# Score products on two 64-row halves of TensorE, with z turned by DMA transposes

## The chip, the cores and the metric

One core of one Trainium2 chip. The metric is the device time of one execution in microseconds (us). Executions of one kernel mostly agree within about 0.3%. Engines: PE is TensorE, DVE is VectorE, ACT is ScalarE, POOL is GpSimd, and SP issues the DMAs. PE writes its products to the memory PSUM; to empty PSUM means to read them from there with ACT or DVE, so that the buffer can be filled again.

## The reference

An attention unit with squared relu scores is followed by a mixer. The shapes are 8 batches, 3136 rows, width 256, and 64 columns of z.

```python
scores = (1 / S) * matmul(z, z.T)              # z: [8, 3136, 64]
x = u * matmul(maximum(scores, 0) ** 2, v)     # u, v: [8, 3136, 256]
h = x.T @ U @ V                                # rank 32
u2 = x + h.T
out = u2 + maximum(u2 @ w_ch1, 0) @ w_ch2      # 256 -> 1024 -> 256
```

## The kernel before

Rows are taken in 25 tiles of 128. For each batch, z is scaled to bf16 (z_bf, whose upper 64 columns are zero), turned on PE against an identity, and cast from PSUM to zzT by ACT. A score product contracts the 128 rows of zzT, of which 64 are zeros.

```python
z_bf = pb2.tile([P, NT, P], BF16, name="z_bf", bufs=1)
nc.gpsimd.memset(z_bf[:, :, dqk:], 0.0)
nc.scalar.mul(out=z_bf[:, :, :dqk], in_=z_raw, mul=zscale)
zzT = pb2.tile([P, S_pad], BF16, name="zzT")              # two buffers
for tg in range(0, NT, 4):
    ...                                                   # four products with ident, one ACT cast to zzT
```

Attention goes by groups of 512 rows (six, and one of 128). A pair of score tiles fills two PSUM banks and is emptied by a relu, one pair in four on DVE and the rest on ACT. DVE then squares it in SBUF. The products with v follow, 100 per group of 512.

```python
ps_s = ps2_pool.tile([P, 2, IGW], FP32, name="ps2")       # three buffers
for jj in range(npair):
    nc.tensor.matmul(out=ps_s[:, jj, :gw],
                     lhsT=zzT[:, (jp + jj) * P : (jp + jj + 1) * P],
                     rhs=zzT[:, g0 : g0 + gw], start=True, stop=True)
if (jp // 2) % 4 == 3:
    nc.vector.tensor_single_scalar(out=attn_sb[...], in_=ps_s[...], scalar=0.0, op=ALU.max)
else:
    nc.scalar.activation(out=attn_sb[...], in_=ps_s[...], func=AF.Relu)
nc.vector.tensor_tensor(out=attn_sb[...], in0=attn_sb[...], in1=attn_sb[...], op=ALU.mult)
```

The kernel is written batch by batch as attention(b), preparation of z and v for b+1, mixer(b). A scheduler sets the final order on each engine and moves work far ahead where buffers allow.

## Time and profile before

| | before |
|---|---|
| time | 1375.08 us |
| PE, DVE, ACT busy | 96%, 52%, 58% |
| attention of a batch (1 to 7), to the start of its last score product | 106.6 us |
| hand-over: from there to the first relu of the mixer (1 to 6) | 13.8 us |
| mixer, from there to its last product | 47.5 us |

The page of a profile gives shares over the whole span. A timeline line gives start, duration (of all merged instructions), engine, source line, operation, output and input, count, and in brackets the idle time before it with what ended it. The last three rows of the table are read from such starts. The lines themselves stand in the prediction.

### The profile page before, as it was taken

The page shows a single profiled execution, that of the slowest core. Times are in us where ns is not written, and L with a number is a line of the kernel's source. Part 1 is how long each engine was busy: PE and PEld are TensorE (multiplying, and loading weights), DVE is VectorE, ACT ScalarE, POOL GpSimd, SP SyncE. Part 2 cuts the span into 40 slices and gives each one's busy share as a digit, 9 for nine tenths or more (in the row PEclk, how much of TensorE's full clock was granted, in tenths as well). Part 3 has the DMA queues.
Part 4 walks back from the last instruction along what each step waited for, and adds up shares of the span by engine and source line. Part 5 has one row for each costly group of instructions (what it writes and reads, how often), then busy time and mean ns, then how long its engine had stood idle before and what let it go on. Part 6 is the DMA issues. An engine that isn't in the chain of part 4 may idle for free.

```text
span 1373.0 us, 22895 instructions
## 1 busy us (share of the span) xinstructions
PE 1317.1 (96%) x9865; PEld 913.3 (67%) x10008; DVE 707.9 (52%) x1104; ACT 792.9 (58%) x976; POOL 23.7 (2%) x41
## 2 busy tenths in 40 slices
PE   3999999999999999999999999999999999999998
PEld 1677666676666766667666676666766667666665
DVE  1776147751477414774157732677217772177721
ACT  6854855557555575556655565655655555455554
POOL 2000000000000000000000000000000000000000
PEclk9999999999999999999999999999999999999999
DMA  9611421124111241111411115111121111111101
GB/s 238 181 32 30 146 71 32 32 64 134 49 32 32 65 146 43 31 32 57 148 49 32 32 49 157 41 32 32 57 102 33 32 32 34 62 34 32 32 32 65
DMA packets 109542, 87.89 MB, mean 64 GB/s; under 512 B 32832, under 2 KB 109120, under 8 KB 109440
## 3 DMA queue, kind: packets, MB, share of 16 engines
q1 hardware_dynamic: 109440, 86.41, 20.7%
q8 instruction: 78, 1.28, 0.4%
q14 instruction: 24, 0.20, 0.0%
HBM read 60.70 MB, written 25.69 MB: 63 GB/s over the span
## 4 chain that ended last, share of the span: by engine, by line
PE 75%; ACT 21%; DMA 2%; issue 1%; DVE 1%; ACTq 0%; SPq 0%; POOL 0%
ACT relu_sb L277 12%; ACT attn_sb L184 4%; ACT u2T_bf L260 3%; ACT zzT L135 2%; DMA v_raw<-in_v_dram 1%; PE ps_6060 L202 0%; PE ps_4297 L202 0%; PE ps_11349 L202 0%; PE ps_7477 L202 0%; PE ps_2188 L202 0%; PE ps_12766 L202 0%; PE ps_11003 L202 0%; PE ps_9240 L202 0%; PE ps_5714 L202 0%; PE ps_2534 L202 0%
## 5 line engine op out<-in xcount | busy, mean ns | idle before, releaser
L202 PEld LDWEIGHTS <-attn_sb 128*128 128x128 bf16 x5000 | 466.9, 98 | 164.3 <-DVE attn_sb L189 61.9
L189 DVE TENSOR_TENSOR attn_sb<-attn_sb 128x1024 bf16<-128x1024 bf16 (+3 forms) x728 | 407.0, 608 | 73.7 <-ACT attn_sb L184 71.4
L169 PEld LDWEIGHTS <-zzT 128*128 128x128 bf16 x1400 | 133.3, 98 | 107.2 <-issue 29.3
L297 PEld LDWEIGHTS <-relu_sb 128*128 128x128 bf16 x1600 | 148.6, 98 | 50.5 <-ACT relu_sb L277 24.0
L270 PEld LDWEIGHTS <-w_bf 128*128 128x128 bf16 x896 | 83.2, 98 | 87.2 <-issue 7.8
L150 ACT CAST v_bf<-v_raw 128x1024 bf16<-128x1024 f32 (+1 forms) x56 | 52.0, 965 | 24.0 <-DMA v_raw<-in_v_dram 15.5
L246 PEld LDWEIGHTS <-x_bf 128*128 128x128 bf16 x400 | 30.3, 97 | 10.7 <-issue 4.5
L128 PEld LDWEIGHTS <-z_bf 128*128 128x128 bf16 x200 | 16.1, 102 | 26.3 <-issue 22.5
L289 PEld LDWEIGHTS <-V_bf 128*128 128x128 bf16 x200 | 19.3, 98 | 6.4
L223 PEld LDWEIGHTS <-U_bf 128*128 128x128 bf16 x200 | 19.6, 98 | 2.2
L212 POOL MEMSET u_sb<- 128x256 f32 x8 | 2.5, 311 | 1047.3 <-DVE x_bf L214 1047.3
L128 PE MATMUL ps_124<-ident,z_bf 128*128 128x128 bf16 x4 | 0.6, 299 | 19.7 <-ACT z_bf L121 19.7
L120 POOL MEMSET z_bf<- 128x1600 bf16 x8 | 11.4, 1431 | 80.8 <-PE ps_6732 L253 13.6
L121 ACT ACTIVATE z_bf<-z_raw 128x1600 bf16<-128x1600 f32 x8 | 12.4, 1550 | 0.0
L253 PEld LDWEIGHTS <-t_sb 128*128 128x128 bf16 x112 | 10.9, 97 | 1.4 <-issue 1.1
L305 DVE TENSOR_TENSOR out_sb<-ps_1522,x_bf 128x512 f32<-128x512 f32 x1 | 0.7, 692 | 16.8 <-PE ps_1522 L297 16.8
L305 DVE TENSOR_TENSOR out_sb<-ps_6811,x_bf 128x512 f32<-128x512 f32 x1 | 0.7, 692 | 16.7 <-PE ps_6811 L297 16.7
L305 DVE TENSOR_TENSOR out_sb<-ps_8574,x_bf 128x512 f32<-128x512 f32 x1 | 0.7, 692 | 16.7 <-PE ps_8574 L297 16.7
L305 DVE TENSOR_TENSOR out_sb<-ps_5048,x_bf 128x512 f32<-128x512 f32 x1 | 0.7, 690 | 16.7 <-PE ps_5048 L297 16.7
L305 DVE TENSOR_TENSOR out_sb<-ps_10337,x_bf 128x512 f32<-128x512 f32 x1 | 0.7, 692 | 16.7 <-PE ps_10337 L297 16.7
L305 DVE TENSOR_TENSOR out_sb<-ps_3285,x_bf 128x512 f32<-128x512 f32 x1 | 0.7, 690 | 16.7 <-PE ps_3285 L297 16.7
L305 DVE TENSOR_TENSOR out_sb<-ps_12100,x_bf 128x512 f32<-128x512 f32 x1 | 0.7, 690 | 16.7 <-PE ps_12100 L297 16.7
(2728 smaller groups left out, 2817.8 us busy)
## 6 DMA issues: line engine op xcount, KB each, us to landing
v_raw<-in_v_dram SPq DMA_DIRECT2D x48, 512.0 KB, 4.8
u_sb<-in_u_dram SPq DMA_DIRECT2D x96, 256.0 KB, 2.6
out_dram<-out_sb SPq DMA_DIRECT2D x96, 256.0 KB, 2.1
z_raw<-in_z_dram SPq DMA_DIRECT2D x8, 768.0 KB, 5.3
wtmp<-in_moe_w_ch_dram SPq DMA_DIRECT2D x4, 512.0 KB, 3.8
v_raw<-in_v_dram SPq DMA_DIRECT2D x8, 64.0 KB, 2.2
u_sb<-in_u_dram SPq DMA_DIRECT2D x8, 64.0 KB, 2.1
out_dram<-out_sb SPq DMA_DIRECT2D x8, 64.0 KB, 2.0
```

Source lines behind the costliest of these rows:

```text
L135: nc.scalar.copy(out=zzT[:, tg * P : (tg + n_in_g) * P], in_=pz[:, : n_in_g * P],)
L150: nc.scalar.copy(out=v_bf[:, c0 : c0 + cn, :], in_=v_raw[:, :cn, :])
L169: nc.tensor.matmul(out=ps_s[:, jj, :gw], lhsT=zzT[:, (jp + jj) * P : (jp + jj + 1) * P], rhs=zzT[:, g0 : g0 + gw], start=True, stop=True,)
L184: nc.scalar.activation(out=attn_sb[:, jp : jp + npair, :gw], in_=ps_s[:, :npair, :gw], func=AF.Relu,)
L189: nc.vector.tensor_tensor(out=attn_sb[:, jp : jp + npair, :gw], in0=attn_sb[:, jp : jp + npair, :gw], in1=attn_sb[:, jp : jp + npair, :gw] ...
L202: nc.tensor.matmul(out=ps_o[:, qq, :], lhsT=attn_sb[:, jt, q * P : (q + 1) * P], rhs=v_bf[:, jt, :], start=(jt == 0), stop=(jt == NT - 1),)
L223: nc.tensor.matmul(out=pt1[:, 0, :], lhsT=U_bf[:, it, :], rhs=x_bf[:, it, :], start=(it == 0), stop=(it == NT - 1),)
L246: nc.tensor.matmul(out=ps_u2[:, db, q * P : (q + 1) * P], lhsT=x_bf[:, it, db * P : (db + 1) * P], rhs=ident, start=(q == 0), stop=False,)
L260: nc.scalar.copy(out=u2T_bf[:, :, c0 : c0 + cw], in_=ps_u2[:, :, :cw])
L270: nc.tensor.matmul(out=ps_m1[:, hh, :cw], lhsT=w1_bf[:, db, ht * P : (ht + 1) * P], rhs=u2T_bf[:, db, c0 : c0 + cw], start=(db == 0), stop ...
L277: nc.scalar.activation(out=relu1_sb[:, hp : hp + 2, :cw], in_=ps_m1[:, :, :cw], func=AF.Relu,)
L297: nc.tensor.matmul(out=ps_f[:, qq, :], lhsT=relu1_sb[:, ht, q * P : (q + 1) * P], rhs=w2_bf[:, ht, :], start=False, stop=(ht == NH - 1),)
```

## The change

A score product needs only 64 rows of the array. The change puts z on both partition halves of zzT and computes the two tiles of a pair on the two halves of the array at the same time. The transposes leave PE and ACT for the DMA queue.

```diff
-        nc.gpsimd.memset(z_bf[:, :, dqk:], 0.0)
         nc.scalar.mul(out=z_bf[:, :, :dqk], in_=z_raw, mul=zscale)
-
+        nc.vector.tensor_copy(out=z_bf[:, :, dqk:], in_=z_bf[:, :, :dqk])
         zzT = pb2.tile([P, S_pad], BF16, name="zzT")
-        for tg in range(0, NT, 4):
-            (PE products with ident, ACT cast to zzT: 14 lines cut)
+        for h0 in range(0, NT, 13):
+            h1 = min(NT, h0 + 13)
+            nc.sync.dma_start_transpose(
+                out=zzT[:, h0 * P : h1 * P].rearrange("p (t r) -> p t r", r=P),
+                in_=z_bf[:, h0:h1, :].rearrange("p t c -> p (t c)"),
             )
...
-                        lhsT=zzT[:, (jp + jj) * P : (jp + jj + 1) * P],
-                        rhs=zzT[:, g0 : g0 + gw],
+                        lhsT=zzT[jj * 64 : jj * 64 + 64, (jp + jj) * P : (jp + jj + 1) * P],
+                        rhs=zzT[jj * 64 : jj * 64 + 64, g0 : g0 + gw],
```

More of the change, by code (lines that the diff above doesn't have):

```diff
@@ L119, in emit_prep @@
         z_bf = pb2.tile([P, NT, P], BF16, name="z_bf", bufs=1)
-        nc.gpsimd.memset(z_bf[:, :, dqk:], 0.0)
         nc.scalar.mul(out=z_bf[:, :, :dqk], in_=z_raw, mul=zscale)
+        nc.vector.tensor_copy(out=z_bf[:, :, dqk:], in_=z_bf[:, :, :dqk])
         zzT = pb2.tile([P, S_pad], BF16, name="zzT")
-        for tg in range(0, NT, 4):
-            n_in_g = min(4, NT - tg)
-            pz = ps1_pool.tile([P, 512], FP32, name="ps1")
-            for q in range(n_in_g):
-                nc.tensor.matmul(
-                    out=pz[:, q * P : (q + 1) * P],
-                    lhsT=z_bf[:, tg + q, :],
-                    rhs=ident,
-                    start=(q == 0),
-                    stop=(q == n_in_g - 1),
-                )
-            nc.scalar.copy(
-                out=zzT[:, tg * P : (tg + n_in_g) * P],
-                in_=pz[:, : n_in_g * P],
+        for h0 in range(0, NT, 13):
[3 more added lines that the diff above has]
+                in_=z_bf[:, h0:h1, :].rearrange("p t c -> p (t c)"),
             )
```

## The prediction

> **What bounds the kernel now.** I read the page first, for shares and for the chain that ended last, then the timeline of single engines over one stretch of attention, then the timeline of ACT where attention hands over to the mixer.
>
> ```profile
> PE 1317.1 (96%) x9865; PEld 913.3 (67%) x10008; DVE 707.9 (52%) x1104; ACT 792.9 (58%) x976; POOL 23.7 (2%) x41
> ...
> PE 75%; ACT 21%; DMA 2%; issue 1%; DVE 1%; ACTq 0%; SPq 0%; POOL 0%
> ACT relu_sb L277 12%; ACT attn_sb L184 4%; ACT u2T_bf L260 3%; ACT zzT L135 2%; DMA v_raw<-in_v_dram 1%; PE ps_6060 L202 0%; PE ps_4297 L202 0%; PE ps_11349 L202 0%; PE ps_7477 L202 0%; PE ps_2188 L202 0%; PE ps_12766 L202 0%; PE ps_11003 L
> ```
>
> This looks PE-bound: 96% busy and 75% of the chain. But the 96% is a count of overlapping, pipelined matmuls and hides a slack of some per cent, and 52% for DVE is an average over attention and mixer. So I looked at DVE between two bursts of PE in the attention of batch 1:
>
> ```profile
> 230.03 0.69 DVE L214 TENSOR_TENSOR x_bf<-ps_2242,u_sb 128x512 bf16<-128x512 f32 x1 [2.36 <-PE ps_2242 L202]
> 231.10 1.22 DVE L177 TENSOR_SCALAR attn_sb<-ps_2312 128x1024 bf16<-128x1024 f32 x1 [0.39 <-PE ps_2312 L169]
> 232.25 3.69 DVE L189 TENSOR_TENSOR attn_sb<-attn_sb 128x1024 bf16<-128x1024 bf16 x6
> 235.86 1.21 DVE L177 TENSOR_SCALAR attn_sb<-ps_2332 128x1024 bf16<-128x1024 f32 x1
> 236.99 2.48 DVE L189 TENSOR_TENSOR attn_sb<-attn_sb 128x1024 bf16<-128x1024 bf16 x4
> 239.40 1.21 DVE L177 TENSOR_SCALAR attn_sb<-ps_2352 128x1024 bf16<-128x1024 f32 x1
> 240.53 1.01 DVE L189 TENSOR_TENSOR attn_sb<-attn_sb 128x512 bf16<-128x512 bf16 x2
> ```
>
> From 230.03 to 241.54 DVE has one gap, 0.39 us. And what PE does then:
>
> ```profile
> 241.60 3.23 PE L202 MATMUL ps_2361<-v_bf,attn_sb 128*128 128x256 bf16 x28
> 244.67 3.22 PE L202 MATMUL ps_2415<-v_bf,attn_sb 128*128 128x256 bf16 x28
> 247.72 0.38 PE L169 MATMUL ps_2485<-zzT 128*128 128x512 bf16 x1
> ```
>
> A burst of 56 products with v starts 0.06 us after DVE's last square, lasts 6.1 us, and then DVE starts its next chain (247.93 to 257.94, without a gap) from the burst's result. A period of two groups of 512 rows is therefore two bursts (241.60 to 247.72, 258.00 to 264.2: 6.1 + 6.2 us) and two DVE chains (11.5 + 10.0 us): 33.8 us, against 34.3 us from the chain (230.24 to 264.55). **In the part of attention in which score products stand, the bound is DVE, with PE close behind it**; the bursts are PE's and hold no score product. The page's 1% for DVE is because the chain credits PE where both end together.
>
> The hand-over to the mixer is ACT's:
>
> ```profile
> 305.63 0.37 ACT L231 CAST t_sb<-ps_3083 128x256 bf16<-128x256 f32 x1 [0.52 <-PE ps_3083 L223]
> 305.90 0.59 ACT L135 CAST zzT<-ps_3119 128x512 bf16<-128x512 f32 x1
> ...
> 308.02 1.02 ACT L260 CAST u2T_bf<-ps_3182 128x1024 bf16<-128x1024 f32 x1
> ...
> 314.55 0.50 ACT L260 CAST u2T_bf<-ps_3254 128x256 bf16<-128x256 f32 x1
> 315.02 1.02 ACT L277 ACTIVATE relu_sb<-ps_3261 128x1024 bf16<-128x1024 f32 x1
> ```
>
> ACT works without a gap from t_sb to the first relu of the mixer, 9.4 us, of which seven zzT casts take 3.26 us (2.11 + 1.15 in the chain).
>
> **What the Trainium skill says.** "TensorEngine Tiling (Array Packing)", PSUM Bottleneck: tiling makes TensorE faster, but not the emptying of PSUM. The trace agrees before the change is made: a pair of score products takes PE 0.43 us (starts 230.04 and 230.47), its relu 0.90 us on ACT or 1.15 us on DVE, and its square 0.61 us on DVE. The same page, Key Properties: a change of tiling mode drains TensorE; no run yet shows it. "Advanced Engine Details and Errata", X-Bar Transpose (TRN2): a DMA transpose is as fast as an ordinary DMA. This trace has no transpose; its nearest is z_raw, 768 KB in 5.3 us from issue to landing. "TensorE: Matmul & The Clock Gate", Why this matters for your kernels: gaps of PE over about 3 us bring the clock back to half. In this trace the first score pairs after the start take 1.06 us, later ones 0.59 us, so it agrees that PE starts slow.
>
> **The change, part by part.**
>
> *Scores.* 150 products of 512 columns per batch, 0.215 us each, are 32 us, 258 us over 8 batches. In halves, at best 129 us of PE go, 9%. But they stand only beside DVE's chains. What DVE waits for PE there is 0.39 us in one chain of two. There are three such periods per batch: 3 x 8 x 0.39 = 9 us at most; I take **-7 us**. Drains: in the built program the score products stand in 396 runs between others (398 before), so some 790 changes of mode; at an assumed 0.1 to 0.2 us, 80 to 160 us of PE time, paid out of the slack of the same stretches: PE has 10.2 us of work in an 11.5 us chain, and 10.2 - 2.7 + about 2 still fits.
>
> *Transposes on PE and their casts.* Seven casts per batch leave ACT's hand-over: -3.26 us, in 7 mixers.
>
> *What takes their place.* The order of instructions in the built program and its semaphores show this; the diff does not. ACT's scaling of z for batch b+3 stands directly before the cast of t_sb in the mixers of batches 0 to 4. z_bf has one buffer, so this scaling waits until the two DMA transposes of batch b+2 have landed, and the first of these waits for the last score product of batch b, because zzT has two buffers. In the trace of before that product ended at 301.45; t_sb began at 305.63. Let T be the time from there to the landing of both transposes. Then t_sb is done at 301.45 + T + 1.56 (scaling) + 0.37. One v_bf cast (1.05) now also stands before the first u2T cast, and seven u2T casts follow (six at 0.91, one of 0.5: 5.9). The first relu of the mixer starts at 310.3 + T instead of 315.02: **a loss of T - 4.7 us** per mixer. The v_bf cast sets a floor: its load is issued at about 304.2, lands 4.8 us later, and gives a relu at 316, +1 us.
>
> T: 13 + 12 tiles of 128x128 bf16 are 819 KB. At the rate of z_raw that is 5.6 us; [...]I expect rather more. My choice is T = 7.5 us, with 5 to 16 possible. Then +2.8 x 5 = **+14 us**. PE sits idle meanwhile for some 5 us and may come back at the half clock; I add **+4 us** in all.
>
> Mixers 5 and 6 have no scaling in that place: -2 and -3 us, **-5 us**.
>
> *Batch 0.* Two scalings, two DVE copies of z (128x1600 bf16, about 1 us by the 0.68 us of a 128x1024 square) and their waits fall into its attention: **+4 us**. At the start the transposes must land before any score product, but before the change the first relu too began only at 26.9 us, 7 us after z_bf was ready: 0 +- 3 us. The other DVE copies fall where DVE sits idle some 17 us in the mixer: nothing. The GpSimd clear of z_bf, off the path, goes.
>
> Sum: -7 + 14 + 4 - 5 + 4 = +10; 1375 + 10 = **1385 us**.
>
> **The rivals.**
>
> *A: PE is the bound.* For it: 96% and 75% of the chain. Then 129 us of scores and 200 transposes at about 0.055 us (11 us) go: 1235 us. Against it: DVE's gapless chains, and a burst that waits for their last square.
>
> *B: the transposes are hidden, as intended.* For it: they are issued a whole attention ahead of the products that read them, and the DMA queues are nearly idle there (1 tenth). Then each of 7 mixers gains about 2 us: 1375 - 7 - 14 = 1354 us at best. Against it: one z_bf buffer with an in-order ACT behind it.
>
> *C: the transposes are slow, or the mode changes dear.* With T = 16 us the loss is 11 us in each of 5 mixers: 1426 us. With 0.3 us per change, PE (7.5 + 16 x 0.3) passes DVE's chain by about 1 us per group of 48: 1425 us. Against it: only the skill's word on transposes.
>
> **Range and chances.** T decides: at its floor the time is some 1366 us, at T = 12 it is 1407. I give 1363 to 1418 us 8 times in 10. More than 2% faster (under 1347.6) needs rival A: 0.05. More than 2% slower (over 1402.6) needs T above 11 us or dear drains: 0.23. Within 2%: 0.72.
>
> **What would show it.** Right: DVE's chains still 10 to 11.5 us between bursts, with the 0.39 us gap gone, and groups of 512 still at 17 us. In mixers 0 to 4 ACT idle before the z_bf scaling until a zzT transpose lands, then t_sb; not in mixers 5 to 7. PE less busy, yet the span about the same. Wrong: periods under 32 us (A), t_sb at its old distance from the last score product (B), transposes landing after 12 us or more, or gaps of PE at each change of mode that DVE waits for (C).

## The result

The changed kernel took 1383.38 us (1382.42 to 1384.33) against 1375.08 us (1375.0 to 1375.15): ratio 1.0065, interval 1.0035 to 1.0094. It is the same within 2%, and slower by 0.65%. Ratios are not quite the ratios of the medians (here 1.0060).

The page of the changed kernel, its lines of busy time and of the chain that ended last:

```profile
PE 1270.0 (92%) x9752; PEld 829.4 (60%) x9808; DVE 713.8 (52%) x1112; ACT 765.8 (55%) x920; POOL 14.0 (1%) x33
...
PE 43%; ACT 27%; DVE 24%; DMA 4%; issue 1%; SPq 1%; ACTq 0%
```

PE is busy 47 us less, and the span is 9.6 us longer. DVE's share of the chain went from 1% to 24%: PE no longer ends together with it. Before, PE had no wait of over 0.15 us for DVE in attention and waited 6.4 us in all for ACT's relus; now it waits 15.2 us for DVE's squares and 26.8 us for the relus. DVE's timeline in batch 1 of the changed kernel, between two bursts of products with v:

```profile
234.33 0.69 DVE L204 TENSOR_TENSOR x_bf<-ps,u_sb 128x512 bf16<-128x512 f32 x1 [2.37 <-PE ps L192]
235.08 1.23 DVE L167 TENSOR_SCALAR attn_sb<-ps 128x1024 bf16<-128x1024 f32 x1
236.22 3.84 DVE L179 TENSOR_TENSOR attn_sb<-attn_sb 128x1024 bf16<-128x1024 bf16 x6
239.97 1.22 DVE L167 TENSOR_SCALAR attn_sb<-ps 128x1024 bf16<-128x1024 f32 x1
241.11 2.49 DVE L179 TENSOR_TENSOR attn_sb<-attn_sb 128x1024 bf16<-128x1024 bf16 x4
243.51 1.22 DVE L167 TENSOR_SCALAR attn_sb<-ps 128x1024 bf16<-128x1024 f32 x1
244.65 1.01 DVE L179 TENSOR_TENSOR attn_sb<-attn_sb 128x512 bf16<-128x512 bf16 x2
```

It is the same chain, 11.3 us in place of 11.5, and the 0.39 us wait for PE before the first relu is gone. The burst follows it, and now PE has waited for DVE:

```profile
245.72 6.29 PE L192 MATMUL ps<-v_bf,attn_sb 128*128 128x256 bf16 x56 [0.44 <-DVE attn_sb L179]
```

The next burst of this kind starts at 279.66: a period of two groups is 33.94 us, where it was 34.31. At the end of attention, the timeline of ACT in batch 0 of the changed kernel, whose last score product starts at 135.71:

```profile
138.04 1.99 ACT L140 CAST v_bf<-v_raw 128x1024 bf16<-128x1024 f32 x2 [1.79 <-PE ps L192]
141.94 1.54 ACT L120 ACTIVATE z_bf<-z_raw 128x1600 bf16<-128x1600 f32 x1 [1.90 <-DMA zzT<-z_bf]
143.38 0.35 ACT L221 CAST t_sb<-ps 128x256 bf16<-128x256 f32 x1
144.66 1.04 ACT L140 CAST v_bf<-v_raw 128x1024 bf16<-128x1024 f32 x1 [0.93 <-DMA v_raw<-in_v_dram]
145.61 6.05 ACT L250 CAST u2T_bf<-ps 128x1024 bf16<-128x1024 f32 x7
151.58 3.77 ACT L267 ACTIVATE relu_sb<-ps 128x1024 bf16<-128x1024 f32 x4
```

ACT waits for a transpose, scales the z of a later batch, and only then casts t_sb, for which PE has been waiting. It then waits once more, for v_raw. SP's timeline at the same time shows why v_raw is late:

```profile
135.97 3.48 SPq L125 DMA_TRANSPOSE zzT<-z_bf  x2
139.55 0.85 SPq L70 DMA_DIRECT2D u_sb<-in_u_dram  x1
140.44 1.02 SPq L70 DMA_DIRECT2D v_raw<-in_v_dram  x2
```

SP spends 3.48 us on issuing two transposes. PE's timeline shows what its 2.4 us of idle time did, in two equal products of that hand-over, the first after the wait and one 4 us later:

```profile
143.79 0.61 PE L243 MATMUL ps<-V_bf,t_sb 128*128 128x512 bf16 x1 [2.38 <-ACT t_sb L221]
...
148.13 0.38 PE L243 MATMUL ps<-V_bf,t_sb 128*128 128x512 bf16 x1
```

The granted clock of PE is 0.50 for the 3.4 us from 143.45 and 1.00 before and after. It fell in the same way in the hand-overs of batches 1, 2 and 4, but not in that of batch 3, where PE stood idle for 2.97 us.

By stages, from the starts in the two timelines (us, changed minus before):

| stage | before | changed | difference, summed |
|---|---|---|---|
| attention of batch 0, with the start | 132.89 | 135.71 | +2.8 |
| attention of batches 1 to 7 | 106.60 each | 106.22 each | -2.6 |
| hand-over, batches 0 to 4 | 14.28, then 13.8 each | 15.87, 16.00, 16.35, 16.39, 17.14 | +12.3 |
| hand-over, batches 5 and 6 | 13.79, 13.80 | 12.59, 11.66 | -3.3 |
| hand-over of batch 7 | 11.55 | 11.66 | +0.1 |
| mixers | 47.5 to 48.8 | 47.7 to 48.0 | +0.3 |

The sum is +9.6 us, the difference of the spans (1382.6 and 1373.0).

### The profile page after: what moved, and what is told of

Its sections match the earlier page's. It is cut to its first block, busy times and chain, and to the rows that moved or that the text cites. A ratio compares the mean times of both kernels' runs of the same rounds, so it can differ in the third digit from the quotient of the medians. Undisturbed runs are those within 1.5% of the kernel's fastest.

```text
span 1382.6 us, 22570 instructions
## 1 busy us (share of the span) xinstructions
PE 1270.0 (92%) x9752; PEld 829.4 (60%) x9808; DVE 713.8 (52%) x1112; ACT 765.8 (55%) x920; POOL 14.0 (1%) x33
## 4 chain that ended last, share of the span: by engine, by line
PE 43%; ACT 27%; DVE 24%; DMA 4%; issue 1%; SPq 1%; ACTq 0%
PE ps L192 25%; DVE attn_sb L179 15%; ACT relu_sb L267 13%; PE ps L287 10%; ACT attn_sb L174 9%; DVE attn_sb L167 8%; ACT u2T_bf L250 3%; PE ps L260 3%; PE ps L159 3%; DMA v_raw<-in_v_dram 2%; DMA zzT<-z_bf 1%; SPq L125 1%; PE ps L279 1%; DVE x_bf L204 1%; PE ps L213 1%
## 5 line engine op out<-in xcount | busy, mean ns | idle before, releaser
L174 ACT ACTIVATE attn_sb<-ps 128x1024 bf16<-128x1024 f32 (+3 forms) x560 | 456.0, 916 | 389.7 <-PE ps L159 388.9
L192 PE MATMUL ps<-v_bf,attn_sb 128*128 128x256 bf16 x5000 | 625.6, 274 | 16.3 <-DVE attn_sb L179 15.2
L159 PE MATMUL ps<-zzT 64*128 64x512 bf16 (+1 forms) x1400 | 229.5, 361 | 60.2 <-ACT attn_sb L174 26.8
L267 ACT ACTIVATE relu_sb<-ps 128x1024 bf16<-128x1024 f32 (+1 forms) x224 | 191.0, 937 | 168.2 <-PE ps L260 168.2
L295 DVE TENSOR_TENSOR out_sb<-ps,x_bf 128x512 f32<-128x512 f32 (+1 forms) x104 | 69.8, 671 | 383.6 <-PE ps L287 383.6
L287 PE MATMUL ps<-w_bf,relu_sb 128*128 128x256 bf16 x1600 | 209.6, 273 | 8.8 <-ACT relu_sb L267 8.2
L260 PE MATMUL ps<-u2T_bf,w_bf 128*128 128x512 bf16 (+1 forms) x851 | 181.4, 355 | 5.7 <-ACT u2T_bf L250 2.4
L167 DVE TENSOR_SCALAR attn_sb<-ps 128x1024 bf16<-128x1024 f32 (+1 forms) x168 | 185.4, 1104 | 0.8
L159 PEld LDWEIGHTS <-zzT 64*128 64x128 bf16 x1400 | 73.5, 94 | 162.5 <-issue 117.3
L204 DVE TENSOR_TENSOR x_bf<-ps,u_sb 128x512 bf16<-128x512 f32 (+1 forms) x104 | 69.8, 671 | 180.6 <-PE ps L192 171.7
L140 ACT CAST v_bf<-v_raw 128x1024 bf16<-128x1024 f32 (+1 forms) x56 | 51.8, 964 | 22.9 <-DMA v_raw<-in_v_dram 13.8
L250 ACT CAST u2T_bf<-ps 128x1024 bf16<-128x1024 f32 (+1 forms) x56 | 47.5, 944 | 3.8 <-PE ps L243 3.7
```

The lines of the kernel that those rows point to most:

```text
L159: nc.tensor.matmul(out=ps_s[:, jj, :gw], lhsT=zzT[jj * 64 : jj * 64 + 64, (jp + jj) * P : (jp + jj + 1) * P], rhs=zzT[jj * 64 : jj * 64 + ...
L167: nc.vector.tensor_single_scalar(out=attn_sb[:, jp : jp + npair, :gw], in_=ps_s[:, :npair, :gw], scalar=0.0, op=ALU.max,)
L174: nc.scalar.activation(out=attn_sb[:, jp : jp + npair, :gw], in_=ps_s[:, :npair, :gw], func=AF.Relu,)
L192: nc.tensor.matmul(out=ps_o[:, qq, :], lhsT=attn_sb[:, jt, q * P : (q + 1) * P], rhs=v_bf[:, jt, :], start=(jt == 0), stop=(jt == NT - 1),)
L204: nc.vector.tensor_tensor(out=x_bf[:, it0 : it0 + nq, :], in0=ps_o[:, :nq, :], in1=u_sb[:, :nq, :], op=ALU.mult,)
L250: nc.scalar.copy(out=u2T_bf[:, :, c0 : c0 + cw], in_=ps_u2[:, :, :cw])
```

## The experiments

The theory: in attention, the emptying of PSUM sets the pace of the stretches with score products, so PE's gain is not seen; the loss is ACT's scaling of z, which waits for transposes ahead of t_sb. Rival A: PE bounds attention. Rival B: the transposes are hidden. Rival C: changes between the 64-row and the 128-row use of the array cost the time. Eleven kernels ran. All results were correct but the two that are wrong on purpose.

### The halves alone

```diff
 (kernel before)
-        nc.gpsimd.memset(z_bf[:, :, dqk:], 0.0)
+        nc.vector.tensor_copy(out=z_bf[:, :, dqk:], in_=z_bf[:, :, :dqk])
-   lhsT=zzT[:, ...], rhs=zzT[:, ...]
+   lhsT=zzT[jj * 64 : jj * 64 + 64, ...], rhs=zzT[jj * 64 : jj * 64 + 64, ...]
```

> Only the half-array score products: z is doubled by DVE but still turned by PE and cast by ACT as before. Theory (DVE bounds the stretches of attention that hold score products): attention of a batch 106.2 us against 106.6 before, last score product to first relu of the mixer 13.8 us as before, whole time 1370 to 1375 us. Rival A (PE bounds attention): half of 258 us of score products goes, near 1250 us. Rival C (changes of array mode cost the time): slower than before, 1380 us or more.

Measured: 1372.11 us (1371.86 to 1372.77), ratio 0.9985 (0.9973 to 0.9998). Attention of a batch is 106.22 us and the hand-over 13.9 us. The change in attention comes from the halves; the whole kernel gains 0.15%. Rival A, which asked for some 1250 us, falls. Nor is it A with the changes of mode eating PE's gain: PE is busy 37 us less than before (1280.3 against 1317.1), but its waits for ACT's relus and DVE's squares in attention rose from 6.4 to 40.3 us.

### The DMA transposes alone

```diff
 (changed kernel)
-        nc.vector.tensor_copy(out=z_bf[:, :, dqk:], in_=z_bf[:, :, :dqk])
+        nc.gpsimd.memset(z_bf[:, :, dqk:], 0.0)
-   lhsT=zzT[jj * 64 : jj * 64 + 64, ...], rhs=zzT[jj * 64 : jj * 64 + 64, ...]
+   lhsT=zzT[:, ...], rhs=zzT[:, ...]
```

> Only the DMA transposes: score products on the full array with zeros in the upper 64 rows, as before. Theory (the scaling of z waits for the transposes ahead of t_sb on ACT): attention 106.6 us, last score product to first relu 15.9 to 17.1 us in the mixers of batches 0 to 4, 12.6 and 11.7 us in those of 5 and 6 as in the changed kernel, whole time 1383 to 1389 us. Rival C: no changes of mode here, so 1375 us or less. Rival B (transposes hidden): 1355 to 1365 us.

Measured: 1386.86 us (1384.74 to 1392.0), ratio 1.0097 (1.0081 to 1.0113). Attention is 106.61 us. The hand-overs of batches 0 to 4 are 16.06, 17.16, 18.94, 16.14 and 17.12 us, one of them well above what was expected; those of 5 and 6 are 12.49 and 11.54. The attention of batch 0 is 4.5 us longer than before. All of the loss is in this part of the change, with no change of mode in the kernel, so C is not its cause; B falls too. The two parts together, -0.15% and +0.97%, make the +0.65% of the whole within the intervals.

### z scaled by DVE

```diff
 (changed kernel)
-        nc.scalar.mul(out=z_bf[:, :, :dqk], in_=z_raw, mul=zscale)
+        nc.vector.tensor_single_scalar(out=z_bf[:, :, :dqk], in_=z_raw, scalar=zscale, op=ALU.mult)
```

> The changed kernel with z scaled by DVE in place of ACT, so that what waits for the transposes no longer stands ahead of t_sb; DVE has nothing to do there. Theory: last score product to first relu falls from 15.9-17.1 to about 12.6 us in the mixers of batches 0 to 4, 5 x 3.7 = 18 us less, 1362 to 1369 us. Rival (the longer hand-over comes from a PE gone slow after its idle time, or from DMA traffic that delays v_raw): hand-over stays above 15 us, 1378 us or more.

Measured: 1364.04 us (1363.43 to 1366.4), ratio 0.9928 (0.9916 to 0.9941). The hand-overs of batches 0 to 4 are 13.08, 12.68, 13.34, 12.96 and 12.59 us, and the attention of batch 0 is 132.91 us, 2.8 us less than in the changed kernel. ACT in the hand-over of batch 0, whose last score product starts at 132.91:

```profile
137.97 0.37 ACT L221 CAST t_sb<-ps 128x256 bf16<-128x256 f32 x1 [0.69 <-PE ps L213]
139.26 3.76 ACT L250 CAST u2T_bf<-ps 128x1024 bf16<-128x1024 f32 x4 [0.92 <-PE ps L213]
142.88 1.08 ACT L140 CAST v_bf<-v_raw 128x1024 bf16<-128x1024 f32 x1
```

The transposes are issued as in the changed kernel (3.5 us of SP for two); what waits for them no longer stands ahead of t_sb, which starts 4.5 to 5.1 us after the last score product in place of 7.4 to 8.7. In the new order the scheduler also moved the late v_bf cast behind four of the u2T casts, so both waits of the hand-over went together, and their shares are not told apart by this run.

### One relu in 13 on DVE

```diff
 (changed kernel)
-                if (jp // 2) % 4 == 3:
+                if jp // 2 == 6:
```

> The changed kernel with one relu in 13 on DVE instead of three; ACT takes the other two. PE's work is the same. Theory (DVE bounds): two relus of 1.15 us leave DVE's chains per group of 512 rows, ACT gains 2 x 0.90 us and comes next; a group goes from 17.0 to between 15.3 and 16 us, 48 groups, whole time 1305 to 1335 us. Rival A (PE bounds attention): no change, 1380 to 1385 us.

Measured: 1419.38 us (1417.72 to 1421.6), ratio 1.0325: the expectation failed, and attention rose to 110.05 us. ACT's timeline of this kernel in batch 1 shows why:

```profile
242.12 10.68 ACT L174 ACTIVATE attn_sb<-ps 128x1024 bf16<-128x1024 f32 x12 [7.06 <-PE ps L159]
259.85 10.68 ACT L174 ACTIVATE attn_sb<-ps 128x1024 bf16<-128x1024 f32 x12 [7.06 <-PE ps L159]
```

ACT's twelve relus are now the gapless chain, 10.68 us. The scheduler also put all of a group's score pairs ahead of a longer burst of products with v (76 in a row), in which ACT sits idle for 7.06 us; 10.68 + 7.06 is the whole group, 17.74 us. So "DVE bounds" was too narrow a name: DVE and ACT share the emptying of PSUM, one hardly behind the other, and the burst adds to it in series. The same PE work as in the changed kernel took 3.8 us more per batch, which again speaks against rival A alone.

### No squares, before and changed (wrong)

```diff
-                nc.vector.tensor_tensor(out=attn_sb[...], in0=attn_sb[...], in1=attn_sb[...], op=ALU.mult)
```

> Wrong on purpose: the kernel before without DVE's squares (0.61 us x 13 per group of 512 rows, nothing added elsewhere). PE then is the only engine near its limit in attention: a group falls from 17.15 us to PE's 16.0 to 16.3 us, 48 groups, 1318 to 1335 us. If PE alone bounded attention already (rival A): 1370 to 1375 us.

> Wrong on purpose: the changed kernel without DVE's squares. Theory (emptying PSUM, by DVE first and ACT just behind, hid the gain of the halves): PE needs 2.7 us less per group than in the run without squares of the kernel before, ACT's 10 relus (9.0 us) stay under it; at least 1 us of the 2.7 shows: 40 us or more below that run after 8 us of longer hand-over are taken into account, 1270 to 1300 us. Rival C (mode changes eat the gain): within 15 us of that run.

Measured: 1382.06 us (ratio 1.0053) for the kernel before without squares, and 1390.06 us (ratio 1.0112) for the changed one. Both expectations failed, and the number set for rival C (within 15 us of each other) came true. Attention stayed at 106.96 and 106.88 us, though DVE was busy only 24% of the time. ACT in the changed kernel without squares:

```profile
233.50 8.85 ACT L174 ACTIVATE attn_sb<-ps 128x1024 bf16<-128x1024 f32 x10 [8.39 <-issue]
250.74 8.84 ACT L174 ACTIVATE attn_sb<-ps 128x1024 bf16<-128x1024 f32 x10 [8.39 <-issue]
```

A group is ACT's chain of 8.85 us and a burst of 80 products, in which ACT idles for 8.39 us: 17.24 us. In the run without squares of the kernel before it is 8.85 + 8.50. The chain has a new owner, the scheduler again lengthened the burst, and the halves are worth 0.1 us per group. It is not rival C that holds them there: PE's waits for ACT rose from 0.30 us a group to 1.35 us. What these three runs point to is the order: **emptying and burst stand one after the other**. After each burst PE fills the three PSUM buffers and then waits for ACT; that the number of buffers is the reason is argued, since no run varied it. The runs do not isolate DVE's share with the order held fixed; every change of DVE's work that I built moved the order.

### Interleaved, before and changed

The products with v of one group are written between the score pairs of the next, 8 after each pair. The work is the same; the loads of u also moved ahead of the products.

```diff
+        for n, _ in enumerate(score_pairs(gi + 1, nxt)):        # one pair of the next group
+            while done < n_av * (n + 1) // pairs:               # 7 or 8 products of this one
+                next(av, None)
+                done += 1
```

> The kernel before with the products with v of one group written between the score pairs of the next (8 after each pair), so that PSUM is emptied through the whole group and there is no burst of 56; same work. Theory: PE then bounds: 16.0 to 16.3 us a group, 1318 to 1335 us. If PE bounded it already: no change, 1370 to 1375 us.

> The same interleaving in the changed kernel: per pair PE has 0.22 us of scores, 8 x 0.107 us of products and two changes of mode. Theory: the halves pay here: 13.7 us a group plus 26 changes of mode at 0.03 to 0.1 us, or DVE's 12.8 us; 14.3 to 16 us a group; 1260 to 1320 us, below the interleaved kernel before by 15 us or more although its hand-over is longer by 8 us. Rival C (a change of mode costs 0.2 us or more): no faster than it.

Measured: 1339.19 us (ratio 0.9743) for the kernel before, 4 us above its expected range, with a group at 16.31 us, and 1350.74 us (ratio 0.9828) for the changed one, whose expectation failed. The order alone is worth 2.6%, which is what the three runs before pointed to. With PSUM emptied throughout, PE bounds, and yet the halves do not pay. PE's timelines, first the interleaved kernel before, then the interleaved changed one:

```profile
241.95 0.59 PE L168 MATMUL ps<-zzT 128*128 128x512 bf16 x2
242.38 1.04 PE L211 MATMUL ps<-v_bf,attn_sb 128*128 128x256 bf16 x8
243.25 0.59 PE L168 MATMUL ps<-zzT 128*128 128x512 bf16 x2
```

```profile
241.60 0.39 PE L158 MATMUL ps<-zzT 64*128 64x512 bf16 x2
241.92 1.05 PE L201 MATMUL ps<-v_bf,attn_sb 128*128 128x256 bf16 x8
242.90 0.39 PE L158 MATMUL ps<-zzT 64*128 64x512 bf16 x2
```

A step is 1.30 us in both. Eight products take 8 x 0.107 = 0.86 us; the rest, 0.44 us, is on the full array the pair itself, and on the halves the pair and two changes of mode. Here rival C holds: the changes of mode eat the whole gain. Where fewer or shorter score products stand between two changes, the halves lose: the step with the odd 25th tile takes 1.30 us against 1.09 us on the full array, and a step of the group of 128 rows 1.14 us against 0.99 us. So attention of a batch is 102.3 us, against 99.7 us in the interleaved kernel before.

### Two pairs at a time

```diff
         for n, _ in enumerate(score_pairs(gi + 1, nxt)):
+            if n % 2 == 0 and n < pairs - 1:
+                continue
             while done < n_av * (n + 1) // pairs:
```

> The interleaved kernel before with two score pairs together and 16 products with v after them. On the full array no change of mode is saved, so the same as with one pair: 1334 to 1344 us.

> The interleaved changed kernel with two score pairs together. With one pair a step took 1.30 us of PE in both interleaved kernels: 8 products at 0.107 us leave 0.44 us, of which the pair needs 0.22; two changes of mode cost the other 0.22. With half the changes a step of two pairs takes 2.38 us in place of 2.60: some 1.4 us less per group, 5 groups per batch, 8 batches: 1285 to 1310 us, well below the interleaved kernels. If not the changes of mode but reading z from half the partitions made the pair slow, the time stays at 1345 to 1355 us.

Measured: 1338.75 us (ratio 0.9741) for the kernel before, and 1302.58 us (ratio 0.9476, 0.946 to 0.9491) for the changed one, both as expected. PE in the changed one:

```profile
244.39 0.61 PE L158 MATMUL ps<-zzT 64*128 64x512 bf16 x4
244.93 1.81 PE L201 MATMUL ps<-v_bf,attn_sb 128*128 128x256 bf16 x15
246.67 0.60 PE L158 MATMUL ps<-zzT 64*128 64x512 bf16 x4
```

A step of two pairs and 15 products is 2.28 us; less 15 x 0.107 that is 0.675 us. With 0.444 us for one pair this gives, for the pair, 0.675 - 0.444 = 0.23 us, and for the two changes of mode 0.444 - 0.23 = 0.21 us, 0.11 us each. From the start of the score products to that of the next product with v it is 0.54 us here and 0.32 us with one pair, which gives 0.22 us for the pair directly. The pairs themselves run at twice the speed; what matters is how many stand together.

### Two pairs at a time, z scaled by DVE

```diff
 (the changed kernel with two pairs at a time)
-        nc.scalar.mul(out=z_bf[:, :, :dqk], in_=z_raw, mul=zscale)
+        nc.vector.tensor_single_scalar(out=z_bf[:, :, :dqk], in_=z_raw, scalar=zscale, op=ALU.mult)
```

> The same with z scaled by DVE. The hand-over of the interleaved changed kernel is 15.4 to 15.8 us in five mixers against 13.8 to 14.8 us in the later ones, so 5 to 15 us less than the two-pair kernel: 1275 to 1300 us, correct, the fastest of all.

Measured: 1302.34 us (ratio 0.9477). It is within neither the expected range nor the expected 5 to 15 us: the same as without. The hand-overs of batches 0 to 4 did fall by 7.1 us in all (15.48 to 14.72 us in batch 0, 18.53 to 14.78 us in batch 4), as expected, but the attention of batch 0 rose by 2.7 us and the early mixers by some 0.58 us each. What the hand-over gained was paid back elsewhere; why is not shown. Either version beats both kernels of the case by 5 to 6%.

## Why the prediction was right

The measured 1383.38 us is 1.6 us from the predicted 1385. The main mechanisms were right, but so close a sum is partly luck: attention gained 4.4 us less than predicted, mixers 5 and 6 gained 1.7 us less, the long hand-overs cost 5.7 us less (with the 4 us for a slow PE), and batch 0 cost 1.2 us less. Step by step:

- **Attention held by the emptying of PSUM.** Right in that the gain is small, but mis-sized: -7 us predicted, -2.6 us measured in batches 1 to 7. The 0.39 us wait is gone and the period is 0.37 us shorter, as the step said. By the end of the sixth group of 512 rows 0.91 us per batch is gained; by the end of the group of 128 rows 0.26 us of it is left. There the pairs are short, and the interleaved runs showed such a step to be 0.15 us dearer on halves; that this is the reason here is likely, not shown. The step's reason was too narrow: DVE was named as the bound with PE close behind. A burst that starts 0.06 us after the last square did not prove a wait for DVE, since PE computed score products until then. The runs with fewer relus on DVE and without squares showed ACT close behind as well, and the burst in series with both.
- **Changes of mode.** 0.1 to 0.2 us was assumed; 0.11 us was measured. In the groups of 512 rows of the changed kernel they were paid from PE's slack, as the step said. That they could eat the whole gain in another order was not foreseen.
- **The scaling of z ahead of t_sb.** Right in mechanism. T was 7.5 us by choice; from the end of the last score product, from which the prediction counts, to the start of the scaling it was 5.8 to 7.0 us. The loss per mixer by T - 4.7 should then have been 1.1 to 2.3 us, 7.3 us in all; it was 1.6 to 3.35, 12.3 us in all against 14. What was mis-sized is the floor: v_raw is not issued 3.0 us after the start of the last score product but 4.7, because SP is busy issuing transposes. So a smaller T and a later v_raw nearly cancelled.
- **PE slow after its idle time.** It happened in four hand-overs of five (0.61 against 0.38 us for a product). The 4 us set aside were too many: in batches 0 to 2 ACT hides it, and in batch 4 the u2T casts waited 0.93 us for PE. That the mixers grew by 0.2 us each is not its doing: they did so in the run with z scaled by DVE too, whose granted clock stayed at 1.00.
- **Mixers 5 and 6** gave -3.3 us against -5, and **batch 0** +2.8 against +4. The doubling of z took DVE 0.59 us, not 1. With z scaled by DVE the +2.8 us was gone, so the scalings on ACT made it, as the step said.
- **The rivals.** A was excluded by the first run, B by the second. C cost the changed kernel at most the 0.65 us per batch lost in the group of 128 rows, but in the interleaved order it is the reason why relief of PSUM alone did not pay.
- **The range.** Its low end, 1366 us at the floor of T, is not what its terms give: without the 4 us for a slow PE they sum to 1367 us with no loss at all, and to 1372 us with the floor of +1 us in five mixers.

## What to carry to other kernels

Before speeding up an engine that is 96% busy, look at one period of its timeline and ask which engine has no gap there; here the products that became faster stood beside chains of DVE and ACT, and the order of work, not the rate of any engine, held the time. Put work that waits for a DMA on an engine whose next instruction nobody needs: that was worth 19 us in the changed kernel, though nothing in the order with two pairs at a time. When the array is used in halves, put several half-array products together, because each change costs about half of what a pair gains here (0.11 of 0.21 us).

## What the Trainium skill lacked or had wrong

- "TensorEngine Tiling (Array Packing)", Key Properties, says that a change of tiling mode drains TensorE and gives no cost. Here it is 0.11 us per change; a pair of 128x512 products on halves takes 0.23 us, against 0.43 us on the full array.
- "Advanced Engine Details and Errata", X-Bar Transpose (TRN2), puts DMA transposes level with ordinary DMAs. For the transfer that is about right here: two transposes of 819 KB together had landed 5.7 to 6.9 us after the first was issued in the hand-overs, while 768 KB of z_raw landed in 5.3 us (6.7 in the changed kernel). That section does not tell of the issue, and the table of sequencer cycles in "DMA: Bandwidth & Descriptors" has none for a transpose of this size: SP took 3.5 us for two transposes (1.35 to 2.6 us each) against 0.4 to 0.5 us for most ordinary loads, and later loads of the queue wait for that.
- "TensorE: Matmul & The Clock Gate", Why this matters for your kernels, warns of PE gaps over about 3 us. Here gaps of 2.2 and 2.4 us were enough: the granted clock was 0.50 for 3.4 us, and products took 0.61 us in place of 0.38. A gap of 2.97 us, in the hand-over of batch 3, did not do it, so the length of the gap alone does not decide.
